# A round's small transfers held until its fifth block's sums are read, in an MLP kernel with spilled squares

## Chip, cores and metric

The kernel runs on one core of a Trainium2 chip. The metric is the device time of one execution in microseconds. The kernel before takes 2218.35 us, the median of three runs (2218.29 to 2221.46).

## The reference

A causal convolution with seven softmaxed taps per head over 8 x 4096 tokens of 192 features, then an MLP with 2048 hidden features whose activation is s * relu(h)^2 + b:

```python
w = np.exp(weight - np.max(weight, axis=-1, keepdims=True))
w = w / (np.sum(w, axis=-1, keepdims=True) + 1e-09)
out = np.einsum('hk,bskhg->bshg', w, x_unf)      # x_unf: seven shifted copies of x
x = out.reshape(B * S, D)                        # 32768 x 192
h = x @ w_in                                     # 192 x 2048
r = np.maximum(h, 0.0)
g = s * (r * r) + b
return (g @ w_out).astype(np.float32)            # 2048 x 192
```

## The kernel before

**Tiling.** Features lie on partitions and tokens on columns. A super-block `n` has 1024 tokens, in two blocks `j` of 512; there are 32. The hidden features come in eight pairs `p` of 2 x 128. A step is one (n, j, p): `first` (line 533) makes h in two banks of PSUM, ACT makes the relu (line 561) and the square (line 569) of 128 x 1024, VectorE makes a rounded copy `qh` (line 571) and the difference `ql` (line 575), and two steps later `second` (line 751) adds the pair's share of output features 0 to 127 from `qh` and `ql`. VectorE also runs the convolution, a tap at a time: line 182 for the first and line 184 for the other six, into `acc` from `xA` (features 0 to 127) or `xB` (the other 64, of two blocks). ACT copies the result to `sA` or `sB` (line 220), VectorE adds the remainder (line 213), and an exchange (lines 196 and 197) swaps the halves of the partitions into `wA` or `wB`, which `first` reads too.

**Rounds.** Output features 128 to 191 are made later from the squares themselves. A round is 48 steps, six blocks, whose squares would be 24 buffers of two steps each; the pool for them, `act`, has 12. So the squares of a round's first three blocks are copied out to DRAM (`away`, line 590), and those of its last three stay. When a round is over, after the second step of the next one, a batch (lines 925 to 941) makes the missing 64 features of all six blocks: first the three that stayed, `near`, then the three that were sent away, `far_off`, whose buffers `call_back` (line 600) loads, 1 MB each, into places that the near blocks' matmuls have freed. `second_B` (line 770) has 64 matmuls a block, about equal shares from its four buffers. There are nine such batches; the tenth, `last_batch` at the program's end, is another function.

**Banks.** The sums of `second` and of `second_B` lie in the pool `ps_o`, two tiles `acc1` and `acc2` with two buffers each, four banks in all. One block takes one bank of each name, so a block's matmuls go to the banks of the block before last. `evict_B` reads a block's sums: ACT once (line 783), then VectorE three times (line 787), and stores 64 x 512 numbers (line 788).

**What sets the order.** PE, ACT and VectorE each keep the order in which the program is written (`in_order`); within a batch so does SP, whose queue issues nearly all transfers and stops at one that has to wait. `convolve(k)` puts up to k taps or other pieces of the convolution at its place in that order; in a batch each block gets WINDOW = 5. `room_for` gives the next free buffer of `act`; who asks first gets the one that is freed first. Before the change the relu of the two steps ahead of a batch asks first, in `step`, and the twelve loads after it. `holding` keeps exchanges back from the first step of a round until the twelve loads are written down.

Of the kernel before, what the change touches and what calls it, by code (L numbers as in the profile page):

```python
# [17 lines left out]
P = 128  # L18
BLK = 512
HB = P // 2  # L20
# [27 lines left out]
def conv_attention_then_squared_relu_mlp(  # L48
# [23 lines left out]
    nc = tc.nc  # L72
    D, T = outT.shape
# [69 lines left out]
                )  # L143


    holding, exchanges = [False], []

    class Tokens:
        def __init__(self, n):
# [39 lines left out]
        @staticmethod  # L189
        def swap(to, of):  # L190

            if holding[0]:
                exchanges.append((to, of))
                return
            to, of = to.bitcast(F32), of.bitcast(F32)
            nc.sync.dma_start(to[0:HB], of[HB:P])
            nc.sync.dma_start(to[HB:P], of[0:HB])

        def places(self, kind, j=0):

# [150 lines left out]
    def room_for(dtype):  # L351
        return act.tile([P, 2, 2, BLK], dtype, name="q")
# [16 lines left out]
    tok = {0: Tokens(0)}  # L369
# [185 lines left out]
    def relu(h):  # L555
        g = count[0]
        count[0] += 1
        if g % 2 == 0:
            two[0] = room_for(F32)
        q = two[0][:, g % 2]  # L560
        nc.scalar.activation(q, h, AF.Relu)  # L561
        return q, g

    def squares(h, cast):
        return square(relu(h), cast)

    def square(at, cast):
        q, g = at
        nc.scalar.activation(q, q, AF.Square)  # L569
        qh, ql = split_place(g)  # L570
        cast(qh, q)  # L571
        return q, qh, ql
# [9 lines left out]
    def place(block):  # L582
        return block // 2, block % 2
# [12 lines left out]
    def call_back(block):  # L596

        for k in range(NPAIR // 2):
            room = room_for(F32)
            nc.sync.dma_start(room.rearrange("p a b c -> p (a b c)"), away[block][:, k])  # L600
            for i in range(2):
                kept[*place(block), 2 * k + i] = room[:, i]
        del away[block]

    def spilled(at):
        k, r = position(at)
        return r < ROUNDS[k] - 2 * RING
# [14 lines left out]
    def put(n, j, p, pair):  # L622
        if n >= OLD:
            kept[n, j, p] = pair[0]
            at = 16 * n + 8 * j + p
            if p % 2 and spilled(at):
                double[at] = two[0]
        queue.append((n, j, p, *lows(*pair)))
# [3 lines left out]
    def banks():  # L632
        return [ps_o.tile([P, BLK], F32, name=f"acc{k}") for k in (1, 2)]
# [130 lines left out]
    def second_B(n, j, accs):  # L764

        for p in range(NPAIR):
            q = kept.pop((n, j, p))
            for r in (slice(0, HB), slice(HB, P)):
                for i in range(2):
                    nc.tensor.matmul(  # L770
                        accs[r.start // HB][i * DB : (i + 1) * DB], WB[r, p, i, :], q[r, i, :],
                        start=p == 0, stop=p == NPAIR - 1, skip_group_check=True,
                    )
        return accs
# [3 lines left out]
    def evict_B(n, j, accs):  # L778

        t0 = n * SUP + j * BLK  # L780
        oB = out_tile(("oB", "oB2", "oC", "oC2", "oA", "oA2")[turn[0] % 6])[0:DB]
        turn[0] += 1
        nc.scalar.activation(  # L783
            oB, accs[0][DB:P], AF.Identity, scale=sb[DB:P], bias=bias[DB:P, 1:2]
        )
        for a in (accs[0][0:DB], accs[1][0:DB], accs[1][DB:P]):
            nc.vector.scalar_tensor_tensor(oB, a, sb[0:DB], oB, op0=ALU.mult, op1=ALU.add)  # L787
        nc.sync.dma_start(outT[P:D, t0 : t0 + BLK], oB)

    def last(n, j, qh, ql):  # L790

# [21 lines left out]
    inputs = [nc.scalar]  # L813

    def pieces():

        def whole(n, kind, j):
            t = tok.setdefault(n, Tokens(n))
            acc = xs.tile([P, BLK], F32, name="acc")
            x = t.xB if kind == "B" else t.xA[:, j * BLK :]  # L820
            for k, _ in enumerate(t.conv(acc, x, tapB if kind == "B" else tapA, BLK)):
                if k < K - 1:
                    yield None
            yield "tapped"
            gate = 16 * n - (0 if j else 8 if kind == "A" else 16)
            while n + j > 1 and now[0] < gate:
                yield "gated"
            once = (n, kind) == (1, "B")
            split = t.split_B_at_once(acc) if once else t.split(kind, j, acc)
            next(split)  # L830
            if kind == "B" and n + 1 < NSUP:
                tok[n + 1] = Tokens(n + 1)
                tok[n + 1].load_B(inputs[0])
            elif j == 1 and n + 1 < NSUP:
                tok[n + 1].load_A(inputs[0])
            yield "after" if once else "cast"
            next(split)
            ready.add((n, kind, j))
            yield None

        order = [(1, "A", 0), (1, "B", 0), (1, "A", 1)]
        for n in range(2, NSUP):
            order += [(n, "B", 0), (n, "A", 0), (n, "A", 1)]
        todo = [whole(*c) for c in order]
        ahead = False
        while todo:
            said = next(todo[0], "over")
            if said == "over":
                todo.pop(0)
                ahead = False  # L850
                continue
            if said in ("cast", "gated") and len(todo) > 1 and not ahead:
                if said == "cast":
                    yield said
                    if not burst[0]:
                        continue
                said = next(todo[1])
                ahead = said == "tapped"
            yield said
# [9 lines left out]
    def convolve(k):  # L869

        k += owed[0]
        owed[0] = 0
        while k > 0:
            said = next(stream, "over")
            if said in ("over", "gated"):
                return
            k -= 1
            burst[0] = k > 0
            if said == "tapped":
                owed[0] = k  # L880
                return
# [40 lines left out]
        convolve(CONV[p] - ahead - between)  # L922


    def batch(k):

        near, far_off = blocks(k)
        inputs[0] = nc.sync
        with in_order(nc.sync):
            for block in far_off:  # L930
                call_back(block)
            holding[0] = False
            while exchanges:
                Tokens.swap(*exchanges.pop(0))
            turn[0] = 0
            for block in near + far_off:
                a = second_B(*place(block), banks())
                convolve(WINDOW)
                evict_B(*place(block), a)
            convolve(0)  # L940
        inputs[0] = nc.scalar

# [25 lines left out]
    waiting = []  # L968

    def step(n, j, p):  # L970
        now[0] = 16 * n + 8 * j + p
        if p == 0:
            if j == 0:
                need(n, "A", 0)
                need(n, "B", 0)
                tok.pop(n - 1)
            else:
                need(n, "A", 1)
        k, r = position(now[0]) if n >= OLD else (0, 0)
        h = first(n, j, p)  # L980
        edge = r if k else None
        if edge == 0:
            holding[0] = True
            convolve(4)
            convolve(3)
            second(*queue.pop(0))
            waiting.append((n, j, p, h))
            return
        if edge == 1:
            second(*queue.pop(0))  # L990
            *at, before = waiting.pop()
            put(*at, squares(before, nc.vector.tensor_copy))
        put(n, j, p, squares(h, nc.scalar.copy if n == OLD and p % 2 else nc.vector.tensor_copy))
        if (n, j) == (1, 1):
            if p < NPAIR - 1:
                column_sums(p + 1)
            convolve(1)
        elif n <= OLD:
            convolve(3 if n == 1 else 2)
        else:  # L1000
            convolve(pace(k, r))
        if (n, j, p) == (2, 0, 0):
            biases()
        elif n == 2 and p % 2 == 0 and unbiased:
            add_bias()
        if (n, j, p) == steps[-1]:
            last_batch(k)
            for item in queue:
                second(*item)
        while queue and len(queue) > LAG + (  # L1010
            queue[0][2] == 0 and queue[0][0] <= OLD and queue[0][:2] not in ((1, 0), (OLD, 1))
        ):
            if (n, j, p) == steps[-1]:
                break
            second(*queue.pop(0))
        if edge == 1:
            batch(k - 1)
        if now[0] - 1 in double:
            with behind(nc.sync):
                send(now[0] - 1)  # L1020
# [63 lines left out]
```

## Time and profile before

| | |
|---|---|
| median of three runs | 2218.35 us |
| the profiled execution's own time | 2218.89 us |
| its span, first to last instruction | 2217.1 us |
| VectorE busy | 1668.1 us, 75% |
| ACT busy | 1298.0 us, 59% |
| bytes moved | 361.44 MB, 163 GB/s over the span |
| `away` written and read back | 120 transfers of 1 MB each way |

In the profile PE is TensorE, PEld its weight loads, DVE VectorE, ACT ScalarE, POOL GpSimd, and SP the engine whose queue (SPq) issues transfers. A row of the timeline reads: start in us from the span's start, duration, engine, line, operation, output and inputs, shapes, count, and in brackets the idle time of the engine just ahead of it with what ended it. A row of the chain reads: start, duration, what, count. In a row of costly groups a bar separates the busy time and the mean of one in ns, and a second bar the idle time ahead of them. Matmuls overlap, and each is drawn with its whole flight, so a busy PE can still be late.

### The profile page before, as it was taken

What the parts mean: (1) busy time and instruction counts of PE and PEld (TensorE: products, weight loads), DVE (VectorE), ACT (ScalarE), POOL (GpSimd) and SP (SyncE); (2) the same over time, 40 slices, a digit from 0 to 9 for tenths busy, and PEclk for the clock granted to TensorE, in tenths of its full rate; (3) what the DMA queues carried; (4) which work ended last, traced back from release to release, by engine and by line L of the source; (5) the groups of instructions that cost most, each with busy time, mean ns of one, the idle gap of its engine ahead of it and who ended that gap; (6) DMA issues with size and microseconds to landing.
All of it is one profiled execution on the core that took longest, in us unless ns stands there. A gap on an engine that the chain in (4) does not pass through costs nothing.

```text
span 2217.1 us, 44853 instructions
## 1 busy us (share of the span) xinstructions
PE 2208.2 (100%) x19334; PEld 1611.6 (73%) x19334; DVE 1668.1 (75%) x2036; ACT 1298.0 (59%) x1390; POOL 108.9 (5%) x81
## 2 busy tenths in 40 slices
PE   9999999999999999999999999999999999999999
PEld 6788875886688578848875885788488758866884
DVE  8888876787678768767876788577768767876763
ACT  8759663665466356636653663566266636644661
POOL 0011000000000000000000000000000000000000
PEclk9999999999999999999999999999999999999999
DMA  5116328523651654185336525541743285246406
GB/s 167 39 28 240 129 58 323 205 73 145 241 204 45 257 179 148 53 318 178 109 102 260 206 71 224 209 158 54 279 182 132 68 306 205 72 169 250 168 20 247
DMA packets 75847, 361.44 MB, mean 163 GB/s; under 512 B 10624, under 2 KB 10880, under 8 KB 44928
## 3 DMA queue, kind: packets, MB, share of 16 engines
q1 hardware_dynamic: 68160, 337.07, 42.0%
q10 hardware_dynamic: 7488, 21.50, 3.3%
q8 instruction: 151, 2.47, 0.5%
q14 instruction: 48, 0.39, 0.1%
HBM read 157.47 MB, written 150.99 MB: 139 GB/s over the span
## 4 chain that ended last, share of the span: by engine, by line
PE 95%; DMA 3%; DVE 1%; ACT 0%; issue 0%; SPq 0%; DVEq 0%; ACTq 0%
PE h L533 47%; PE acc L751 29%; PE acc L770 14%; DMA q<-away 3%; PE h L770 2%; PE acc L697 2%; PE acc L667 0%; PE acc L673 0%; DVE acc L184 0%; PE acc L675 0%; PE acc L674 0%; DVE ql L575 0%; PE acc L666 0%; DMA xA<-in_xA 0%; PE acc L669 0%; DVE q L313 0%
## 5 line engine op out<-in xcount | busy, mean ns | idle before, releaser
L561 ACT ACTIVATE q<-h 128x1024 f32<-128x1024 f32 x512 | 525.9, 1027 | 502.5 <-PE h L533 495.5
L575 DVE TENSOR_TENSOR ql<-q,qh 128x1024 fp32r<-128x1024 f32 x498 | 611.1, 1227 | 54.6 <-ACT qh L571 4.9
L571 DVE CAST qh<-q 128x1024 fp32r<-128x1024 f32 x482 | 334.1, 693 | 343.5 <-ACT q L569 340.5
L751 PE MATMUL acc<-qh,W 64*128 64x512 f32 x3816 | 587.9, 386 | 0.0
L569 ACT ACTIVATE q<-q 128x1024 f32<-128x1024 f32 x512 | 543.6, 1062 | 16.0
L533 PE MATMUL h<-sB,W 64*128 64x512 f32 x1536 | 430.1, 386 | 0.0
L533 PE MATMUL h<-wB,W 64*128 64x512 f32 x1536 | 430.1, 386 | 0.0
L533 PE MATMUL h<-sA,W 64*128 64x512 f32 x3024 | 426.1, 387 | 0.0
L533 PE MATMUL h<-wA,W 64*128 64x512 f32 x3024 | 424.9, 386 | 0.0
L751 PEld LDWEIGHTS acc<-qh,W 64*128 64x128 f32 x3816 | 357.4, 184 | 76.0 <-issue 0.8
L770 PE MATMUL acc<-q,WB 64*64 64x512 f32 x3520 | 380.9, 590 | 3.4 <-DMA q<-away 3.4
L751 PE MATMUL acc<-ql,W 64*128 64x512 f32 x1908 | 371.6, 386 | 0.0
L533 PEld LDWEIGHTS h<-sA,W 64*128 64x128 f32 x3024 | 282.4, 184 | 66.6 <-issue 7.3
L533 PEld LDWEIGHTS h<-wA,W 64*128 64x128 f32 x3024 | 283.2, 184 | 59.6
L770 PEld LDWEIGHTS acc<-q,WB 64*64 64x64 f32 x3520 | 134.0, 133 | 245.0 <-issue 230.5
L533 PEld LDWEIGHTS h<-sB,W 64*128 64x128 f32 x1536 | 282.5, 184 | 30.7 <-issue 0.2
L533 PEld LDWEIGHTS h<-wB,W 64*128 64x128 f32 x1536 | 282.5, 184 | 30.2
L184 DVE SCALAR_TENSOR_TENSOR acc<-xA,tap,acc 128x512 f32<-128x512 f32 x378 | 292.3, 773 | 6.3
L751 PEld LDWEIGHTS acc<-ql,W 64*128 64x128 f32 x1908 | 178.7, 184 | 37.5
L787 DVE SCALAR_TENSOR_TENSOR outs<-acc,sb,outs 64x512 f32<-64x512 f32 x165 | 123.1, 746 | 93.1 <-ACT outs L783 84.3
L783 ACT ACTIVATE outs<-acc,bias,sb 64x512 f32<-64x512 f32 x55 | 42.6, 775 | 256.8 <-PE acc L770 256.8
L760 POOL TENSOR_TENSOR outs<-outs 128x512 f32<-128x512 f32 x59 | 95.2, 1613 | 1749.9 <-ACT outs L759 1749.9
(141 smaller groups left out, 858.0 us busy)
## 6 DMA issues: line engine op xcount, KB each, us to landing
away<-q SPq DMA_DIRECT2D x120, 1024.0 KB, 5.9
q<-away SPq DMA_DIRECT2D x120, 1024.0 KB, 11.1
wA<-sA SPq DMA_DIRECT2D x124, 256.0 KB, 3.7
wB<-sB SPq DMA_DIRECT2D x62, 256.0 KB, 4.0
outT<-outs SPq DMA_DIRECT2D x59, 256.0 KB, 2.3
xA<-in_xA ACTq DMA_DIRECT2D x23, 515.0 KB, 3.5
outT<-outs SPq DMA_DIRECT2D x62, 128.0 KB, 4.9
xB<-in_xB ACTq DMA_DIRECT2D x21, 259.0 KB, 3.0
```

What stands on the lines that cost most here:

```text
L184: nc.vector.scalar_tensor_tensor(acc, src, w[:, k : k + 1], acc, op0=ALU.mult, op1=ALU.add)
L533: nc.tensor.matmul(h[:, i, :], w_in(w, p, chunk[0], rows), chunk[part], start=start, stop=stop)
L561: nc.scalar.activation(q, h, AF.Relu)
L569: nc.scalar.activation(q, q, AF.Square)
L571: cast(qh, q)
L575: nc.vector.tensor_tensor(ql, q, qh.bitcast(F32), op=ALU.subtract)
L697: nc.tensor.matmul(accs[to + 2 * i][0:cols], w(f, r), q[r, f % 2, :], start=start and f == 0, stop=stop and f == NF - 1,)
L751: nc.tensor.matmul(accs[i], w(f, r), q[r, f % 2, :], start=f == 0 and lo == 0, stop=f == ends[i] and lo == 2,)
L760: nc.gpsimd.tensor_tensor(o, o, o2, op=ALU.add)
L770: nc.tensor.matmul(accs[r.start // HB][i * DB : (i + 1) * DB], WB[r, p, i, :], q[r, i, :], start=p == 0, stop=p == NPAIR - 1, skip_group_c ...
L783: nc.scalar.activation(oB, accs[0][DB:P], AF.Identity, scale=sb[DB:P], bias=bias[DB:P, 1:2])
L787: nc.vector.scalar_tensor_tensor(oB, a, sb[0:DB], oB, op0=ALU.mult, op1=ALU.add)
```

## The change

Every transfer that is asked for while `holding` is set goes into a list `later`: exchanges, the next `xB` and the stores of the 64 features. `let_go` empties the list after the fifth block of the batch has been read out, the fifth block's store first. The two waiting steps' squares, until now written ahead of the batch, come inside it, after the first block's sums are read, and between them stand the calls for buffers: the loads of the first far block ask for four, then the squares for one, then the other eight loads.

```diff
+    def put_off(transfer):
+        if holding[0]:
+            later.append(transfer)
+        else:
+            transfer()
+
+    def let_go():
+        holding[0] = False
+        for transfer in later[-1:] + later[:-1]:
+            transfer()
+        later.clear()
...
-            if holding[0]:
-                exchanges.append((to, of))
-                return
             to, of = to.bitcast(F32), of.bitcast(F32)
-            nc.sync.dma_start(to[0:HB], of[HB:P])
-            nc.sync.dma_start(to[HB:P], of[0:HB])
+
+            @put_off
+            def exchange():
+                nc.sync.dma_start(to[0:HB], of[HB:P])
+                nc.sync.dma_start(to[HB:P], of[0:HB])
...
-        nc.sync.dma_start(outT[P:D, t0 : t0 + BLK], oB)
+        put_off(lambda: nc.sync.dma_start(outT[P:D, t0 : t0 + BLK], oB))
...
-                tok[n + 1].load_B(inputs[0])
+                put_off(lambda: tok[n + 1].load_B(inputs[0]))
...
-    def batch(k):
+    def batch(k, meanwhile):
...
-            for block in far_off:
-                call_back(block)
-            holding[0] = False
-            while exchanges:
-                Tokens.swap(*exchanges.pop(0))
+            call_back(far_off[0])
             turn[0] = 0
             for block in near + far_off:
                 a = second_B(*place(block), banks())
+                if block == near[0]:
+                    evict_B(*place(block), a)
+                    meanwhile()
+                    for away_block in far_off[1:]:
+                        call_back(away_block)
                 convolve(WINDOW)
-                evict_B(*place(block), a)
+                if block != near[0]:
+                    evict_B(*place(block), a)
+                if block == far_off[-2]:
+                    let_go()
             convolve(0)
...
         if edge == 1:
             second(*queue.pop(0))
-            *at, before = waiting.pop()
-            put(*at, squares(before, nc.vector.tensor_copy))
+
+            def puts():
+                *at, before = waiting.pop()
+                put(*at, squares(before, nc.vector.tensor_copy))
+                put(n, j, p, squares(h, nc.vector.tensor_copy))
+
+            batch(k - 1, puts)
+            return
...
-        if edge == 1:
-            batch(k - 1)
```

PE keeps its order, and so does POOL. In what follows the numbers in names count up in the order in which tiles are asked for.

VectorE, around the first batch, before. `acc1_3823` and `acc2_3824` are the first block's sums, `acc1_3866` and `acc2_3867` the second's; `q_3784` holds the squares of the two waiting steps.

```order
L184 SCALAR_TENSOR_TENSOR acc_3732<-xB_3251,tap_58,acc_3732 128x512 x2
L571 CAST qh_3787<-q_3784 128x1024
L575 TENSOR_TENSOR ql_3788<-q_3784,qh_3787 128x1024
L571 CAST qh_3793<-q_3784 128x1024
L575 TENSOR_TENSOR ql_3794<-q_3784,qh_3793 128x1024
L184 SCALAR_TENSOR_TENSOR acc_3732<-xB_3251,tap_58,acc_3732 128x512 x4
L787 SCALAR_TENSOR_TENSOR outs_79<-acc1_3823,sb_62,outs_79 64x512
L787 SCALAR_TENSOR_TENSOR outs_79<-acc2_3824,sb_62,outs_79 64x512 x2
L182 TENSOR_SCALAR acc_3905<-xA_3730,tap_58 128x512
L213 TENSOR_TENSOR sB_3900<-acc_3732,sB_3900 128x512
L184 SCALAR_TENSOR_TENSOR acc_3905<-xA_3730,tap_58,acc_3905 128x512 x3
L787 SCALAR_TENSOR_TENSOR outs_79<-acc1_3866,sb_62,outs_79 64x512
```

The same place with the change, where the first block's sums are `acc1_3792` and `acc2_3793`, the second's begin with `acc1_3863`, and the squares lie in `q_3830` (lines are 12 higher).

```order
L196 SCALAR_TENSOR_TENSOR acc_3732<-xB_3251,tap_58,acc_3732 128x512 x2
L799 SCALAR_TENSOR_TENSOR outs_79<-acc1_3792,sb_62,outs_79 64x512
L799 SCALAR_TENSOR_TENSOR outs_79<-acc2_3793,sb_62,outs_79 64x512 x2
L583 CAST qh_3833<-q_3830 128x1024
L587 TENSOR_TENSOR ql_3834<-q_3830,qh_3833 128x1024
L583 CAST qh_3839<-q_3830 128x1024
L587 TENSOR_TENSOR ql_3840<-q_3830,qh_3839 128x1024
L196 SCALAR_TENSOR_TENSOR acc_3732<-xB_3251,tap_58,acc_3732 128x512 x4
L194 TENSOR_SCALAR acc_3900<-xA_3730,tap_58 128x512
L225 TENSOR_TENSOR sB_3897<-acc_3732,sB_3897 128x512
L196 SCALAR_TENSOR_TENSOR acc_3900<-xA_3730,tap_58,acc_3900 128x512 x3
L799 SCALAR_TENSOR_TENSOR outs_79<-acc1_3863,sb_62,outs_79 64x512
```

The three reads of the first block's sums went ahead of the casts and differences of the squares; everything from these casts to the read of the second block stands behind them as it did. ACT has the same exchange of places: line 783 for the first block now stands ahead of the four rows of lines 561 and 569.

SP, the first loads of the same batch, before:

```order
L761 DMA outT<-outs_79 128x512
L600 DMA q_3797<-away_1825 128x2048
L600 DMA q_3799<-away_1825 128x2048
L600 DMA q_3801<-away_1825 128x2048
L600 DMA q_3803<-away_1825 128x2048
L600 DMA q_3805<-away_2186 128x2048
```

and with the change:

```order
L773 DMA outT<-outs_79 128x512
L612 DMA q_3784<-away_1825 128x2048
L612 DMA q_3786<-away_1825 128x2048
L612 DMA q_3788<-away_1825 128x2048
L612 DMA q_3790<-away_1825 128x2048
L612 DMA q_3843<-away_2186 128x2048
```

The rows are the same, but the squares' buffer was asked for ahead of all loads (`q_3784`) and now comes fifth (`q_3830`), between the fourth load's and the fifth's.

SP behind the loads, before, with the numbers left out:

```order
L600 DMA q<-away 128x2048 x12
L196 DMA wA<-sA 64x1024
L197 DMA wA<-sA 64x1024
L788 DMA outT<-outs 64x512
L174 DMA xB<-in_xB 128x518
L196 DMA wB<-sB 64x1024
L197 DMA wB<-sB 64x1024
L788 DMA outT<-outs 64x512 x5
L590 DMA away<-q 128x2048 x3
```

and with the change:

```order
L612 DMA q<-away 128x2048 x12
L800 DMA outT<-outs 64x512
L208 DMA wA<-sA 64x1024
L209 DMA wA<-sA 64x1024
L800 DMA outT<-outs 64x512
L186 DMA xB<-in_xB 128x518
L208 DMA wB<-sB 64x1024
L209 DMA wB<-sB 64x1024
L800 DMA outT<-outs 64x512 x4
L602 DMA away<-q 128x2048 x3
```

One store, the fifth block's, moved from among the last five to directly behind the loads; it waits for that block's read, and the other transfers stand behind it in the queue.

More of the change, by code (lines that the diff above doesn't have):

```diff
@@ L143, in in_order @@
                 )
-    holding, exchanges = [False], []
+    holding, later = [False], []
+    def put_off(transfer):
[8 more added lines that the diff above has]
+        later.clear()
     class Tokens:
```

## The prediction

> **What bounds the kernel now.** I read the page first, then the chain of work that ended last, then the timeline of each engine through one round's second half, and last the way of single transfers.
>
> ```profile
> PE 2208.2 (100%) x19334; PEld 1611.6 (73%) x19334; DVE 1668.1 (75%) x2036; ACT 1298.0 (59%) x1390; POOL 108.9 (5%) x81
> L770 PE MATMUL acc<-q,WB 64*64 64x512 f32 x3520 | 380.9, 590 | 3.4 <-DMA q<-away 3.4
> ```
>
> The first row says that TensorE has matmuls in flight for the whole span; the second that the batches (line 770) are the only large group before which it sits idle, for transfers that bring squares back. So time can be won only where PE waits for `away`, and whatever makes PE wait anew is added in full: nothing downstream has room to hide it.
>
> How much is there to win? The chain gives the start of each of the nine batches that the change touches:
>
> ```profile
> 328.14 41.36 PE acc L770 x384
> ...
> 532.97 22.52 PE acc L770 x208
> 555.51 17.83 DMA q<-away
> ...
> 738.78 22.52 PE acc L770 x208
> ...
> 944.90 41.36 PE acc L770 x384
> ...
> 1149.73 41.36 PE acc L770 x384
> ...
> 1354.56 22.52 PE acc L770 x208
> ...
> 1560.76 22.52 PE acc L770 x208
> ...
> 1766.10 41.36 PE acc L770 x384
> 1807.45 2.29 PE h L533 x18
> 1970.92 41.42 PE acc L770 x384
> ```
>
> An undisturbed batch takes 41.36 us, 6.89 for each of its six blocks and 1.72 for each of its 24 buffers. From start to start the rounds take 204.83, 205.81, 206.12, 204.83, 204.83, 206.20, 205.34 and 204.82 us. Four of them, just those whose batch the chain breaks with a transfer, are longer than 204.82, by 0.99, 1.30, 1.38 and 0.52: **4.2 us in all** that PE loses to late loads. That is the whole of what can be gained, 0.19% of the span.
>
> Why these loads are late is seen on SP and in two of the twelfth loads, the second batch's and the last one's:
>
> ```profile
> 331.80 19.20 SPq L600 DMA_DIRECT2D q<-away  x12
> 351.10 1.04 SPq L196 DMA_DIRECT2D wA<-sA  x1
> ...
> L600 SPq DMA_DIRECT2D q<-away x1: 319/319/319, 555.5 to 555.5; - x1
> DMA to landing us min/median/max: 17.8/17.8/17.8
> ...
> L600 SPq DMA_DIRECT2D q<-away x1: 319/319/319, 2188.5 to 2188.5; - x1
> DMA to landing us min/median/max: 14.9/14.9/14.9
> ```
>
> PE needs the twelfth buffer 23 x 1.72 = 39.6 us after a batch began. In the second batch it landed at 555.5 + 17.8 = 573.3, which is 40.3 after 532.97; there the exchanges are issued 0.4 us behind it and share its DMA engines. The last batch, which has nothing but a few stores behind its loads and starts them one buffer earlier, had it at 2203.4, about 35.8 after its start. With the change nothing is issued behind the loads until PE is through the fifth block, as in the last batch.
>
> **The change part by part.** *Transfers held back.* No instruction is added or removed, only moved. The loads lose their company. The first one takes the first buffer instead of the second, but stands behind the store of line 761 in SP's queue, so I count nothing for its earlier start. The last batch says that the twelfth load then lands some 3 us before it is needed. I take **-4.2 us**; the bounds are -4.2 and 0, since rounds without a break show that PE cannot gain more.
>
> What waits on SP behind the held store: both exchanges, the next `xB`, five stores, then the copies to `away`. The exchanges end in `wA`, which the eighth step of the new round reads, some six steps of 3.4 us after the batch's end, and a `wA` transfer takes this long:
>
> ```profile
> wA<-sA SPq DMA_DIRECT2D x124, 256.0 KB, 3.7
> 399.75 1.53 DVE L182 TENSOR_SCALAR acc<-xB,tap 128x512 f32<-128x512 f32 x1
> ```
>
> The fifth block ends at 328.14 + 5 x 6.89 + 3.4 (the wait worked out below) = 366.0 and is read by about 369; ten issues of about 1 us each (the exchange's above took 1.04) are out by 380; `wA` is wanted at about 393 and `xB` at 403, 3.4 later than the row. I take zero. Without this cover each late microsecond would cost one per round, 9 in all.
>
> *The squares go behind the first block.* This is the part that decides. VectorE works in order, and before, it filled PE's first block with casts and differences of the two waiting steps:
>
> ```profile
> 326.48 0.62 ACT L220 CAST sA<-acc 128x512 fp32r<-128x512 f32 x1 [4.33 <-DVE acc L184]
> ...
> 330.09 1.02 ACT L561 ACTIVATE q<-h 128x1024 f32<-128x1024 f32 x1 [0.50 <-PE acc L770]
> ...
> 333.14 1.06 ACT L569 ACTIVATE q<-q 128x1024 f32<-128x1024 f32 x1
> 335.21 0.78 ACT L783 ACTIVATE outs<-acc,bias,sb 64x512 f32<-64x512 f32 x1 [1.00 <-PE acc L770]
> 339.32 0.62 ACT L220 CAST sB<-acc 128x512 fp32r<-128x512 f32 x1 [3.34 <-DVE acc L184]
> ...
> 327.13 0.69 DVE L213 TENSOR_TENSOR sA<-acc,sA 128x512 fp32r<-128x512 f32 x1 [0.29 <-ACT sA L220]
> ...
> 332.23 0.69 DVE L571 CAST qh<-q 128x1024 fp32r<-128x1024 f32 x1 [2.96 <-ACT q L569]
> ...
> 336.18 3.11 DVE L184 SCALAR_TENSOR_TENSOR acc<-xB,tap,acc 128x512 f32<-128x512 f32 x4
> 339.20 2.38 DVE L787 SCALAR_TENSOR_TENSOR outs<-acc,sb,outs 64x512 f32<-64x512 f32 x3
> 341.50 0.47 DVE L182 TENSOR_SCALAR acc<-xA,tap 128x512 f32<-128x512 f32 x1
> 341.89 0.68 DVE L213 TENSOR_TENSOR sB<-acc,sB 128x512 fp32r<-128x512 f32 x1
> 342.49 2.32 DVE L184 SCALAR_TENSOR_TENSOR acc<-xA,tap,acc 128x512 f32<-128x512 f32 x3
> 344.84 2.38 DVE L787 SCALAR_TENSOR_TENSOR outs<-acc,sb,outs 64x512 f32<-64x512 f32 x3
> ```
>
> A block's sums take two of the four accumulator banks, so the fourth block's matmuls go where the second block's sums lie, and PE cannot start it, at 328.14 + 3 x 6.89 = 348.8, before VectorE has read these. It read them from 344.84 to 347.22: a margin of 1.6 us. Now the same chain with the change, for this round:
>
> 1. The squares' buffer is the fifth instead of the first, freed four buffers, 6.89 us, later. The first relu starts at 330.09 + 6.89 = 336.98, free of the first block's read on ACT (335.21 to 335.99).
> 2. The first cast on VectorE follows it as before: 332.23 + 6.89 = 339.12, and the four `xB` taps start at 336.18 + 6.89 = 343.07 and end at 346.18. The read of the first block moves ahead, to about 336.0 to 338.4, into a stretch in which VectorE now waits anyway (it stands still from 332.23 - 2.96 = 329.3 on), so moving it out of its old place saves nothing.
> 3. After the taps: line 182 from 346.09; the cast to `sB` on ACT from 346.21 (339.32 less the 339.29 at which the taps ended, again); line 213 can start 0.65 after that cast, as in the pair 326.48 and 327.13, at 346.86, where without that wait it would start at 346.48. Then 342.49 - 341.89 = 0.60 and 344.84 - 342.49 = 2.35 as before: the second block's read starts at 349.81 and ends at 352.19, **5 us later than before**.
> 4. PE's first two matmuls of the fourth block need one bank, free at about 350.6; the third, due at 349.0, needs the other bank and so the end of all three reads, 352.2. With 0.15 us to restart, the block is **3.4 us late**.
>
> Later blocks have their banks in time: after 352.2 three taps (2.3) and a read (2.4) free the third block's banks by 357, and the fifth block, which takes them, begins at 352.2 + 6.7 = 358.9. So it costs one wait of 3.4 us in each batch, and the same in all nine, since the order is the same in each: **+30.4 us**. Bounds: without step 3's extra wait and with quicker hand-overs 2.6 us, 23.4 in all; with the 0.3 that PE's restarts and slow reads can add here and there, and somewhat more, 3.9 us, 35.1 in all. The middle has its rows, so I take it. PE's wait also moves the need of every called-back buffer 3.4 us later, a second reason why no load is late any more.
>
> The profiled execution took 2218.89 us, a span of 2217.1 and 1.8 around it; 2218.89 - 4.2 + 30.4 = 2245.1. It lies 0.54 above the median of the runs, so for the median I say **2244.5 us**.
>
> **A clock that follows idleness.** Does a wait of 3.4 us also cost clock? Two stretches of 3.41 us and the end, as stretch, length, busy time and count of PE, weight loads, VectorE, ACT and POOL, granted clock, DMA share and GB/s:
>
> ```profile
> 1393.78:1397.19 3.41, 2.24 (x20) 0.51 (x16) 0.00 (x0) 0.00 (x0) 0.00 (x0) 1.00 0.91 221
> 2212.98:2216.39 3.41, 0.56 (x3) 0.13 (x1) 0.88 (x2) 0.00 (x0) 0.00 (x0) 1.00 0.39 115
> 2216.39:2217.10 0.71, 0.00 (x0) 0.00 (x0) 0.00 (x0) 0.00 (x0) 0.00 (x0) 0.50 0.00 0
> ```
>
> With PE busy 2.24 of 3.41 us the granted clock stayed at 1.00; after a stretch with 0.56 it went to 0.50. In the new wait PE has the two early matmuls and the third block's last ones in flight, about 1.0 of 3.41 by the 590 ns of line 770's row, between the two. If the clock halves, a stretch of the 2.9 us that lie between the last matmul and the drop would lose 1.45 us a batch, 13 in all: 2257.5. The Trainium skill ("TensorE: Matmul & The Clock Gate", Part 1) says that the gate halves the clock after an idle window of about 3.4 us, free-running, and opens it after a busy one; by that a drop would cost 1.7 a batch, 15 in all, and, read strictly, the two early matmuls would prevent it. The end of this trace agrees with the halving; that a broken gap suffices, no row shows.
>
> **Rivals.**
> - *The wait for the bank is short or none*, 7%: the place is the fourth block's first matmuls; it decides at 348.8, so VectorE would have to be 3.4 us quicker, for instance if the two casts ran before the first block's read after all. For it: VectorE idles some 10 us there. Against it: the fifth buffer is freed by PE alone, at 336.7 at the earliest. Then only the loads count: 2218.35 - 4.2 = 2214.1.
> - *The wait just balances the gain*, under 1 us a batch, 3%: 2214 to 2222.
> - *The loads stay late all the same*, so that the held transfers bring nothing, 5%. For it: DMA engines stay full with 12 MB alone. Against it: the last batch. 2248.7.
> - *The clock falls in the waits*, 13%: 2249 if in a third of them, 2257.5 in all.
>
> **How the numbers follow.** The forecast has 72%, at 2237.5 (-4.2 + 23.4) to 2249.3 (-4.2 + 35.1). The late-load rival adds 4.2 to its upper end, the clock rival with up to half of the waits some 6.5 to the likeliest; I say 2237 to 2254. Left out are the first two rivals and the clock's worse half. Two thousandths, 4.4 us, is about what a measurement of this kernel can tell from no change. Faster 6%, within 4%, slower 90%.
>
> **What would show it.** In the profile after: no idle time of PE for `away`; a wait of PE or its weight loads at the fourth block for the read on VectorE, 1.5 to 3.4 us, in nine batches; that read some 5 us later than before; batches of about 44.7 us; the twelfth load landing within 38 us of the start; SP issuing the held store about 41 us after the start. I am wrong if PE goes from the third block to the fourth without a break, if the wait falls on other blocks, or if the steps after a batch grow longer because an exchange comes late.

## The result and the profile after

| | before | after |
|---|---|---|
| median of four runs | 2218.32 us | 2246.70 us |
| lowest to highest | 2217.87 to 2221.46 | 2244.96 to 2247.28 |
| profiled execution, span | 2218.89, 2217.1 | 2247.28, 2245.5 |

The ratio is 1.0124, with a 95% interval of 1.0106 to 1.0141: the change makes the kernel 1.2% slower. 2244.5 had been forecast, in a range of 2237 to 2254. One run of the kernel before, among those beside experiment 9, took 3488.38 us at a granted clock of 0.602 and is left out of the median there.

The profile page of the changed kernel, engines and the batches' group:

```profile
PE 2220.7 (99%) x19334; PEld 1612.3 (72%) x19334; DVE 1668.6 (74%) x2036; ACT 1297.8 (58%) x1390; POOL 108.9 (5%) x81
L782 PE MATMUL acc<-q,WB 64*64 64x512 f32 x3520 | 393.3, 593 | 19.6 <-DVE outs L799 19.6
```

No engine's work has grown, apart from PE's matmuls in flight. The 3.4 us of idle time for `away` are gone from the group's last column, and 19.6 us for VectorE's reads (line 799, formerly 787) have taken their place. The list of waits, for PE and for its weight loads (total us, times, longest), says that they fall 18 times, twice in each of the nine batches. The 2.18 us a batch are less than PE loses, as the chain shows below, because a matmul in flight counts as busy:

```profile
PE acc L782 <- DVE outs L799: 19.6, 18, 1.6
...
PEld acc L782 <- DVE outs L799: 35.4, 18, 2.5
```

The chain gives the batches (start, duration, what, count), and behind some of them the first matmuls of the next step, line 545:

```profile
328.09 20.77 PE acc L782 x192
352.10 22.51 PE acc L782 x188
374.61 2.28 PE h L545 x18
538.06 20.77 PE acc L782 x192
562.07 20.82 PE acc L782 x188
582.89 2.27 PE h L545 x18
746.32 20.77 PE acc L782 x192
...
1787.66 20.77 PE acc L782 x192
...
1995.91 20.77 PE acc L782 x192
...
2196.02 7.03 PE acc L782 x64
```

Each batch now breaks after 192 matmuls, three of its six blocks, and goes on with the last 188; the four between are those that find a free bank. From the start to the next step the second one takes 582.89 - 538.06 = 44.83 us, against 41.36 undisturbed. From start to start the rounds take 208.25 to 208.29 us, **3.44 more** than the 204.82 of before; only the first takes 209.97, another **1.70** more. So the sum closes: 9 x 3.44 + 1.70 - 4.2 = 28.5, and 2218.89 + 28.5 = 2247.4, against 2247.28.

VectorE's timeline in the first batch, the place that the prediction worked out:

```profile
335.96 2.38 DVE L799 SCALAR_TENSOR_TENSOR outs<-acc,sb,outs 64x512 f32<-64x512 f32 x3 [6.75 <-ACT outs L795]
339.04 0.69 DVE L583 CAST qh<-q 128x1024 fp32r<-128x1024 f32 x1 [0.71 <-ACT q L581]
...
342.92 3.10 DVE L196 SCALAR_TENSOR_TENSOR acc<-xB,tap,acc 128x512 f32<-128x512 f32 x4
345.94 0.48 DVE L194 TENSOR_SCALAR acc<-xA,tap 128x512 f32<-128x512 f32 x1
346.70 0.69 DVE L225 TENSOR_TENSOR sB<-acc,sB 128x512 fp32r<-128x512 f32 x1 [0.29 <-ACT sB L232]
347.31 2.32 DVE L196 SCALAR_TENSOR_TENSOR acc<-xA,tap,acc 128x512 f32<-128x512 f32 x3
349.67 2.38 DVE L799 SCALAR_TENSOR_TENSOR outs<-acc,sb,outs 64x512 f32<-64x512 f32 x3
```

VectorE stands empty for 6.75 us, then works nearly without a break, and its read of the second block, the last row, starts at 349.67 where it started at 344.84 before. On PE's timeline of the first and the second batch the fourth block waits for just that read:

```profile
350.46 1.07 PE L782 MATMUL acc<-q,WB 64*64 64x512 f32 x4 [1.62 <-DVE outs L799]
352.10 22.51 PE L782 MATMUL acc<-q,WB 64*64 64x512 f32 x188 [0.56 <-DVE outs L799]
...
560.44 1.08 PE L782 MATMUL acc<-q,WB 64*64 64x512 f32 x4 [1.62 <-DVE outs L799]
562.07 20.82 PE L782 MATMUL acc<-q,WB 64*64 64x512 f32 x188 [0.56 <-DVE outs L799]
```

The 188 matmuls are the same work in both batches, yet they take 22.51 us in the first and 20.82 in the second. The difference, 1.69, is the first round's extra. The clock explains it: stretches of the first batch and of the second, as length, busy time and count of PE, weight loads, VectorE, ACT and POOL, granted clock, DMA share and GB/s.

```profile
349.27:352.68 3.41, 1.66 (x12) 0.50 (x16) 3.24 (x5) 0.39 (x1) 0.00 (x0) 1.00 1.01 428
352.68:356.09 3.41, 3.41 (x24) 1.05 (x20) 3.17 (x6) 0.00 (x0) 0.00 (x0) 0.50 1.03 432
557.48:560.89 3.41, 1.79 (x18) 0.38 (x12) 3.20 (x5) 0.77 (x1) 0.00 (x0) 1.00 1.00 420
560.89:564.31 3.42, 2.86 (x28) 0.86 (x28) 3.28 (x6) 0.00 (x0) 0.00 (x0) 1.00 1.03 434
```

After a stretch with PE busy 1.66 us the clock was 0.50 for one stretch, and after one with 1.79 it stayed at 1.00, as it did in the seven batches that follow.

Last, SP in the first batch, and the twelfth load of the second one, issued at 564.0:

```profile
331.34 24.26 SPq L612 DMA_DIRECT2D q<-away  x12
370.23 0.49 SPq L800 DMA_DIRECT2D outT<-outs  x1
...
L612 SPq DMA_DIRECT2D q<-away x1: 319/319/319, 564.0 to 564.0; - x1
...
DMA to landing us min/median/max: 11.0/11.0/11.0
```

It landed at 575.0, 37.0 after the batch began, where it had been 40.3. In all nine batches the twelfth load comes 36.3 to 37.0 after the start.

### The profile page after: what moved, and what is told of

It is laid out like the page before. It is cut to its first block, busy times and chain, and to the rows that moved or that the text cites. A ratio compares the mean times of both kernels' runs of the same rounds, so it can differ in the third digit from the quotient of the medians.

```text
span 2245.5 us, 44788 instructions
## 1 busy us (share of the span) xinstructions
PE 2220.7 (99%) x19334; PEld 1612.3 (72%) x19334; DVE 1668.6 (74%) x2036; ACT 1297.8 (58%) x1390; POOL 108.9 (5%) x81
## 4 chain that ended last, share of the span: by engine, by line
PE 97%; DVE 2%; ACT 0%; DMA 0%; issue 0%; SPq 0%; DVEq 0%; ACTq 0%
PE h L545 46%; PE acc L763 29%; PE acc L782 17%; PE h L782 2%; PE acc L709 2%; DVE outs L799 1%; PE acc L679 0%; ACT outs L795 0%; PE acc L685 0%; PE acc L687 0%; DVE acc L196 0%; PE acc L686 0%; DVE ql L587 0%; PE acc L678 0%; DMA xA<-in_xA 0%; PE acc L681 0%
## 5 line engine op out<-in xcount | busy, mean ns | idle before, releaser
L782 PE MATMUL acc<-q,WB 64*64 64x512 f32 x3520 | 393.3, 593 | 19.6 <-DVE outs L799 19.6
```

The costliest lines, as they stand in the source:

```text
L782: nc.tensor.matmul(accs[r.start // HB][i * DB : (i + 1) * DB], WB[r, p, i, :], q[r, i, :], start=p == 0, stop=p == NPAIR - 1, skip_group_c ...
```

## The experiments

The theory: the squares' new place empties VectorE ahead of the first block's read, the delay is carried in order to the second block's read, and PE pays for it at the fourth block; holding the transfers costs nothing. The rivals: the held transfers or the loads' new order have a part in the loss; PE's wait comes from the read's place behind its taps alone; the clock needs a whole idle stretch to fall. Each kernel below is the changed one with the edit shown, and computes the whole result. "Before" is the kernel before, run beside it on the same chip.

**1. The transfers held, the squares where they were.**

```diff
-            call_back(far_off[0])
+            for block in far_off:
+                call_back(block)
...
-                if block == near[0]:
-                    evict_B(*place(block), a)
-                    meanwhile()
-                    for away_block in far_off[1:]:
-                        call_back(away_block)
                 convolve(WINDOW)
-                if block != near[0]:
-                    evict_B(*place(block), a)
+                evict_B(*place(block), a)
...
-            batch(k - 1, puts)
+            puts()
+            batch(k - 1)
```

> One half of the change alone: exchanges, input and stores are held until the fifth block is read, but the two waiting steps' squares stay ahead of the batch and take the first buffer, as before. My theory (the whole loss is the fourth block's wait for the second block's banks, which comes from the squares' move; holding the transfers removes the late loads): about 2214.1 us, that is 4.2 below before, no idle time of PE for the loads, batches of 41.4 us, twelfth load landed within 38.5 us of a batch's start. Rival 1 (the held transfers themselves delay later steps): 2240 or more. Rival 2 (loads are late from their own 12 MB, not from company): 2218, with the same four batches broken.

Measured: 2214.43 us (2213.94 to 2214.72, 11 runs), before 2216.84 (15 runs), ratio 0.9987 (0.9978 to 0.9996). The chain of this kernel:

```profile
327.88 41.36 PE acc L782 x384
532.71 41.36 PE acc L782 x384
...
1966.50 41.36 PE acc L782 x384
```

All nine batches are undisturbed, 204.83 apart, and the twelfth loads land 37.4 to 38.0 after the start, where before they came at 38.5 to 40.8. Holding the transfers costs nothing and wins 2.4 us against the median beside it.

**2. The squares' move alone.** Nothing is held past the loads:

```diff
-        for transfer in later[-1:] + later[:-1]:
+        for transfer in later:
...
                     for away_block in far_off[1:]:
                         call_back(away_block)
+                    let_go()
...
-                if block == far_off[-2]:
-                    let_go()
```

> The other half alone: the squares go behind the first block's read with the fifth buffer, and the transfers are let go right behind the twelve loads, as before. My theory: the wait of 3.47 us stands in all nine batches (+31.2 us); the late loads no longer show, because PE needs them 3.47 us later: 2245.3 us plus 1.7 for each drop of the clock. Rival (the late loads add to it): about 2249.5 us, with idle time of PE for loads.

Measured: 2246.88 us (2245.07 to 2249.61, 4 runs), before 2216.84, ratio 1.0137 (1.0121 to 1.0152). The list of waits has the same row as the whole change:

```profile
PE acc L782 <- DVE outs L799: 19.6, 18, 1.6
```

The first batch has the same single stretch at half clock. So the whole loss comes from the squares' move. The loads land 38.7 to 40.3 us after the start; with the fourth block late PE wants them only at 43.0 (39.6 + 3.4). Within the changed kernel, holding the transfers therefore wins nothing: the new wait covers the late loads by itself.

**3. The second block read ahead of its taps**, with the whole change otherwise kept:

```diff
+                if block == near[1]:
+                    evict_B(*place(block), a)
                 convolve(WINDOW)
-                if block != near[0]:
+                if block not in near[:2]:
                     evict_B(*place(block), a)
```

> The whole change, and the second block's sums are read ahead of that block's five pieces of convolution instead of behind them. My theory: the second block's read ends near 20.5 us after the batch's start instead of 24, so that PE finds the banks free: no wait for VectorE, no late loads, 2214.1 us, and no drop of the clock. Rival (the wait comes from something else, such as the later squares as such): 2235 to 2247 us. A rival within it: the read ends after 20.9 and a wait of some tenths is left in each batch, 2215 to 2218 us.

Measured: 2228.88 us (2228.6 to 2229.25, 5 runs), before 2216.84, ratio 1.0054 (1.0042 to 1.0067). The expectation missed by 14.8 us. VectorE's timeline in the second batch, and then PE's:

```profile
552.15 2.38 DVE L799 SCALAR_TENSOR_TENSOR outs<-acc,sb,outs 64x512 f32<-64x512 f32 x3
...
555.45 4.67 DVE L196 SCALAR_TENSOR_TENSOR acc<-xA,tap,acc 128x512 f32<-128x512 f32 x6
560.15 2.38 DVE L799 SCALAR_TENSOR_TENSOR outs<-acc,sb,outs 64x512 f32<-64x512 f32 x3
...
562.96 4.69 DVE L196 SCALAR_TENSOR_TENSOR acc<-xA,tap,acc 128x512 f32<-128x512 f32 x6
567.68 4.79 DVE L799 SCALAR_TENSOR_TENSOR outs<-acc,sb,outs 64x512 f32<-64x512 f32 x6
```

```profile
570.12 7.08 PE L782 MATMUL acc<-q,WB 64*64 64x512 f32 x60 [0.43 <-DVE outs L799]
```

The wait at the fourth block is gone, but VectorE is still full from one read to the next, 8.0 us from 552.15 to 560.15 and 7.5 to the next, while a block lasts 6.89. The fourth block's read, the first half of the last VectorE row, ends at about 570.06, and there the sixth block's fifth matmul starts. The delay had only been handed on, at a smaller price: 14.5 us of span for the nine batches over the first experiment (2227.1 - 2212.6), 1.6 each. I had costed one read and not the work that VectorE still owed.

**4. The same, with nothing held** (the edits of 2 and 3 together):

> As the kernel with the second block's read first, but the transfers are not held: they go right behind the twelve loads. Theory A (the earlier start of the first four loads is enough to have the twelfth in time): 2214 us and no idle time of PE for loads. Theory B (the company behind the twelfth load is what makes it late): 2216 to 2218 us, with some batches broken as before.

Measured: 2229.12 us (2228.82 to 2229.3, 5 runs), before 2216.84, ratio 1.0055 (1.0042 to 1.0068). PE waits for no load here, although the twelfth come 38.2 to 40.3 after the start, because the wait for the banks makes the need later as in 2. On whether the held transfers are needed it says nothing, being covered.

**5. The squares' buffer asked for ahead of all loads**, as before, and the squares still written behind the first block's read:

```diff
-            call_back(far_off[0])
...
-                    for away_block in far_off[1:]:
+                    for away_block in far_off:
                         call_back(away_block)
```

> The whole change, but the squares' buffer is asked for ahead of all loads again: they still stand behind the first block's read, and take the first buffer. It parts the wait of 3.47 us into its two causes. My theory: the relu then follows the first block's read on ACT at 7.9 us after the batch's start instead of waiting for the fifth buffer until 8.9; the chain on VectorE comes 1.0 us earlier, and the wait is 2.5 us a batch: 2218.3 - 4.2 + 9 x 2.5 = 2236.6 us, with fewer or no drops of the clock. Rival (the fifth buffer is the main cause): under 2225. Rival (the place behind the read is all of it): 2245.

Measured: 2236.85 us (2236.74 to 2236.97, 4 runs), before 2218.14 (21 runs), ratio 1.0084 (1.0068 to 1.0099). VectorE's timeline in the second batch, and PE's:

```profile
542.98 2.38 DVE L799 SCALAR_TENSOR_TENSOR outs<-acc,sb,outs 64x512 f32<-64x512 f32 x3 [6.74 <-ACT outs L795]
545.28 0.68 DVE L583 CAST qh<-q 128x1024 fp32r<-128x1024 f32 x1
```

```profile
556.55 1.08 PE L782 MATMUL acc<-q,WB 64*64 64x512 f32 x4 [0.68 <-DVE outs L799]
```

The first cast no longer waits for ACT, whose square has long been there, and PE's first wait shrinks from 1.62 to 0.68. The span is (2235.0 - 2212.6) / 9 = 2.5 us per batch over the first experiment, against 3.44. So 0.94 of the 3.44 come from the fifth buffer on top of the 2.5 of the place behind the read, which leaves VectorE empty all the same.

**6. A longer wait.** Two of the third block's pieces of convolution go ahead of the second block's read:

```diff
-                convolve(WINDOW)
+                convolve(WINDOW + {1: 2, 2: -2}.get((near + far_off).index(block), 0))
```

> The whole change, with two more taps ahead of the second block's read and two fewer ahead of the third's: the wait grows by two taps, 1.55 us, to 5.0 us in each of nine batches, still broken by two early matmuls. It asks what the clock costs. Without any drop of the clock: 2214.2 + 9 x 5.0 = 2259 us. Theory (a stretch of the clock's window of 3.41 us in which PE is busy less than half halves the clock for the next one, 1.7 us lost each time): with 5.0 us nearly every batch has such a stretch, eight or nine drops, 2273 to 2275 us. Rival (drops come from unbroken idleness of 3.4 us alone): none or one, 2259 to 2261 us.

Measured: 2274.7 us (2273.66 to 2276.1, 4 runs), before 2218.14, ratio 1.0254 (1.024 to 1.0268). PE's timeline and the stretches in the first batch:

```profile
351.61 1.31 PE L782 MATMUL acc<-q,WB 64*64 64x512 f32 x4 [3.19 <-DVE outs L799]
```

```profile
348.91:352.32 3.41, 0.71 (x4) 0.19 (x4) 3.20 (x5) 0.32 (x1) 0.00 (x0) 1.00 1.01 425
352.32:355.73 3.41, 3.09 (x14) 0.80 (x16) 3.20 (x6) 0.00 (x0) 0.00 (x0) 0.50 1.01 425
355.73:359.14 3.41, 3.41 (x36) 1.15 (x32) 3.27 (x6) 0.00 (x0) 0.00 (x0) 1.00 1.01 420
```

The stretches in the ninth batch:

```profile
2038.51:2041.92 3.41, 1.50 (x16) 0.31 (x8) 3.27 (x6) 0.91 (x2) 0.00 (x0) 1.00 1.01 420
2041.92:2045.33 3.41, 1.56 (x10) 0.41 (x14) 3.24 (x5) 0.00 (x0) 0.00 (x0) 1.00 1.01 428
2045.33:2048.74 3.41, 3.41 (x22) 1.05 (x18) 3.20 (x6) 0.00 (x0) 0.00 (x0) 0.50 1.01 425
```

The read comes 1.57 us later in the batch than with the change (350.81 - 327.66 against 349.67 - 328.09), which makes 3.44 + 1.57 = 5.0; the span shows (2272.1 - 2212.6) / 9 = 6.6 a batch. The rest is the clock: nine stretches at 0.50, one in each batch of the profiled execution. PE's longest idle time is 3.2 us, and in the stretch ahead of the drop it still had work, 0.71 us in the first batch and 1.08 to 1.56 in the others. That the clock falls only after a whole idle stretch doesn't hold; had it stayed up, the time would have been near 2259.

**7. Every block read ahead of its taps**, the whole change otherwise kept:

```diff
-                convolve(WINDOW)
-                if block != near[0]:
-                    evict_B(*place(block), a)
+                else:
+                    evict_B(*place(block), a)
+                convolve(WINDOW)
```

> The whole change, and every block's sums are read ahead of that block's pieces of convolution, not only the first two's. With the second's alone read first, the wait went to the fifth and sixth blocks, 1.66 us in all, since VectorE's arrears stayed and only the order of paying changed. My theory: with all reads first no read stands behind more than one block's pieces, every bank is free in time and batches take 41.4 us: 2214.4 us, the same as with the squares left ahead of the batch. Rival (the arrears of 5 us must show somewhere): 2222 to 2230 us.

Measured: 2214.36 us (2213.98 to 2214.89, 11 runs), before 2218.14, ratio 0.9983 (0.9975 to 0.9992). VectorE's timeline in the second batch, from the second block's read to the fourth's:

```profile
550.77 2.38 DVE L799 SCALAR_TENSOR_TENSOR outs<-acc,sb,outs 64x512 f32<-64x512 f32 x3
...
556.41 2.38 DVE L799 SCALAR_TENSOR_TENSOR outs<-acc,sb,outs 64x512 f32<-64x512 f32 x3
...
561.27 2.38 DVE L799 SCALAR_TENSOR_TENSOR outs<-acc,sb,outs 64x512 f32<-64x512 f32 x3 [0.25 <-ACT outs L795]
```

By the fourth read VectorE waits for ACT again: it has caught up. What it owes is now taps, for which nobody waits in the batch, and PE has no wait for a read any more.

**8. Taps in the empty time.** The first block's pieces of convolution go ahead of its read; the squares stay behind it, with the fifth buffer:

```diff
                 if block == near[0]:
+                    convolve(WINDOW)
                     evict_B(*place(block), a)
...
-                convolve(WINDOW)
                 if block != near[0]:
+                    convolve(WINDOW)
                     evict_B(*place(block), a)
```

> The whole change, but the first block's five pieces of convolution stand ahead of its read, as before the change, and so fill the time in which VectorE stands idle for PE's first block; the squares stay behind the read with the fifth buffer. My theory (the wait is VectorE's empty time, paid back three blocks later): the second block's read starts at 18.3 us after the batch's start and ends at 20.7, just in time; no wait or up to 0.3 us a batch: 2214 to 2217 us. Rival (the late squares as such hold the next steps or the banks back): 2230 us or more.

Measured: 2214.6 us (2214.36 to 2214.97, 11 runs), before 2218.14, ratio 0.9982 (0.9974 to 0.9991). VectorE's timeline in the second batch:

```profile
534.33 3.22 DVE L196 SCALAR_TENSOR_TENSOR acc<-xB,tap,acc 128x512 f32<-128x512 f32 x3
540.25 2.38 DVE L799 SCALAR_TENSOR_TENSOR outs<-acc,sb,outs 64x512 f32<-64x512 f32 x3 [2.70 <-ACT outs L795]
...
550.55 2.38 DVE L799 SCALAR_TENSOR_TENSOR outs<-acc,sb,outs 64x512 f32<-64x512 f32 x3
```

The empty time falls from 6.75 to 2.70 us, and the second block's read ends at 552.93, just before PE wants its banks (532.37, the batch's start in the chain, plus 3 x 6.89 is 553.04). The loss is gone with the squares still in their new place: it was the empty time, not the squares as such; the fifth buffer alone costs next to nothing.

**9. As 7, with nothing held** (the edits of 2 and 7 together):

> The kernel with all reads first, but the transfers are let go right behind the twelve loads, as before the change: of the change's help for the loads only the earlier start of the first four is left, with no wait for banks to cover a late one. Theory (both help: with company and an early start the twelfth load landed 38.2 to 40.3 us after a batch's start in the kernel with the second block read first, and PE needs it at 39.6): most batches in time, none to two of nine broken, 2214.4 to 2216 us. Rival (the early start does nothing for the twelfth load): four or more batches broken, 2217 to 2219 us.

Measured: 2214.82 us (2214.44 to 2216.1, 11 runs), before 2217.04 (15 runs), ratio 0.999 (0.9981 to 0.9999). The list of waits has one row for loads:

```profile
PEld acc L782 <- DMA q<-away: 2.8, 6, 0.7
```

The twelfth loads land 38.4 to 39.5 after the start, just within the 39.6 that PE allows. Here the first four loads start one buffer earlier than before and the exchanges still run beside them, and PE loses next to nothing to late loads in this execution.

Experiments 1, 7 and 8 are faster than both kernels, by 0.13 to 0.18% of the one before, with intervals that end below 1. The runs of each lie within some 0.9 us of each other, where those of the kernel before, beside the first of them, go from 2215.31 to 2219.99.

## Why the prediction held, step by step

**The gain.** -4.2 us: no batch breaks for a load any more, as forecast, and experiment 1 has nine batches of 41.36. The 4.2 are those of one execution, of 2218.89 us; against the medians of the kernel before, which vary, experiments 1, 7 and 8 win 2.4 to 3.8. I gave the whole to the held transfers and counted nothing for the earlier start. Held alone, with the loads one buffer later, is enough (experiment 1, landing at 37.4 to 38.0), and the earlier start brings 1 us more (36.3 to 37.0 with both). Early and not held was only just enough in 9, with 2.8 us of weight loads' waits: in 2 and 4, with the same early start, twelfth loads came as late as 40.3, after the 39.6 of an undisturbed batch, and only the new wait covered them. So that the early start alone is enough is shown for 9 and not in general. In the changed kernel the new wait alone would also have done (2).

**The held transfers' lateness.** Zero was right: the rounds grow by 3.44 us, the wait and nothing else, since from a batch's end to the next one's start it is 746.32 - 582.89 = 163.43 us, against 204.82 - 41.36 = 163.46. SP issued the held store at 370.23, 42.1 us after the start, one later than said; but this batch had the drop of the clock, and in the second it was 578.51 - 538.06 = 40.5.

**The chain through VectorE.** First cast 339.12 forecast, 339.04 measured; taps from 343.07 and 342.92; the remainder (line 213 before, 225 now) at 346.86 and 346.70; the second block's read from 349.81 and 349.67. The wait for the copy to `sB`, the term that the lower bound left out, is in the trace with 0.29 us. VectorE's empty time, some 10 us in the first rival, was 6.75 and 0.71, 7.5 in all. Experiments 5 and 8 show that the two causes that I named together weigh differently: the fifth buffer adds 0.94 of the 3.44, and next to nothing once the empty time is filled (8, batches of 41.43 against 41.36); the empty time ahead of the read makes the rest.

**PE's wait.** 3.38 us a batch forecast (30.4 / 9), 3.44 measured; the early matmuls at about 350.6 and 350.46, the rest at 352.35 and 352.10. Nine times the same, at the fourth block only, and later blocks in time, as worked out. The rivals of no wait or of a balance are out, and so are the loads staying late.

**The clock.** This was the term left out of the sum, and the size that was off. I had estimated PE's busy time in the wait at about 1.0 of 3.41 us; 1.66 and 1.79 were measured. The stretch ahead of the drop holds the four early matmuls (1.07 us) and the first 0.58 us after the wait, from 352.10 to its end at 352.68, which I had not counted. So the wait stands near the edge: one drop in nine batches, 1.70 us, where I had put 1.45 on a drop, in the profiled execution. With 9 x 0.06 from the wait it makes up the 2.2 by which the forecast fell short of the median (2246.70 - 2244.5). Three of the four runs lie at 2246.66 to 2247.28 and one at 2244.96. One drop more or less would explain that, and the mean granted clocks agree: 0.999 in the three and 1.000 in the fourth, while one drop takes 1.70 of 2245.5 us, 0.0008. The slowest run of experiment 2, 2249.61 us, has 0.997. That the clock fell once and not in all nine batches I had not worked out, only given chances; with nine drops the time would have been near 2260, outside the range. To that extent the number was luck. The Trainium skill ("TensorE: Matmul & The Clock Gate", Part 1) has the clock halve after an idle window of about 3.4 us and open again after a busy one. The trace agrees on the length (0.50 for 3.41 us) and, with 1.70 us, on the estimate of 1.7 for a drop that I had worked out from it, and differs on the condition: the stretch ahead of the drop was 49% busy here, and 21 to 46% in experiment 6. The measurement decides.

## What to carry to other kernels

An engine that works in order carries a delay on until its own free time has eaten it: when work is moved behind something that comes later, count the empty time that it leaves, and follow the engine's debt up to the first instruction that someone else waits for. Moving that one instruction ahead hands a part of the debt on (experiment 3, 1.6 of 3.44 us); filling the empty time (8), or letting the work that nobody waits for come last throughout (7), removes it. A change of two parts is best taken apart: here one was worth 2 to 4 us of gain, and the other cost 31.

## What the runs showed of the hardware

The granted clock can halve for one stretch of 3.41 us without TensorE being idle for so long. In the changed kernel's first batch 1.75 us of idle time in one stretch, with 1.66 us busy, were enough; 1.79 us busy in the other eight were not. In experiment 6 the nine drops came after stretches with 0.71 to 1.56 us busy. Each drop lasted one stretch. It cost 1.7 us, and less only in experiment 6's first three batches (1.2 in the first), where it began while PE still waited.

The stretches lie on a grid of their own. In experiment 6 the batches start 211.05 to 211.57 us apart, but the drops 211.63 each time, 62 stretches of 3.413 us. The changed kernel's rounds of 208.26 us are 61.0 stretches, so that each batch from the second on meets them in the same phase, and one that is spared is spared again. The first round, longer by its own drop, was 61.5 (209.97 us): it put the second batch half a stretch off the phase in which the first had met them.

Where the edge lies isn't settled. The busy time is drawn with whole flights, and it doesn't sort the cases cleanly: in the ninth batch of experiment 6 a stretch with 1.50 us was not followed by a drop, and the next one, with 1.56, was.
